# Moving the last pair's first addition, six splits and two copies at the seam of attention and experts

## The chip, the cores and the metric

The kernel runs on one core of a Trainium2 chip. The metric is device microseconds of one execution. The core has TensorE (PE in the rows, PEld for its weight loads), VectorE (DVE), ScalarE (ACT), GpSimd (POOL) and SyncE (SP, which here only issues transfers). Each engine takes its instructions in the order in which they stand, and waits where an operand or a buffer isn't there yet.

## The reference

Attention with bounded scores over 4 batches of 12 heads, then a layer of 8 experts in which each of the 1792 tokens goes to the expert with the largest logit.

```python
# q, k, v: (4, 12, 448, 64); cap = 30
scores = scale * np.matmul(q, k.transpose(0, 1, 3, 2))
scores = cap * np.tanh(scores / cap)
attn = np.exp(scores - max);  attn = attn / (sum(attn) + 1e-09)
out = np.matmul(attn, v)
# x = out, tokens by 768; 8 experts, w1 (768 x 1024), w2 (1024 x 768)
logits = xn @ en.T / tau            # both normalized
expert_idx = np.argmax(logits, axis=1)
probs = softmax(logits);  gate_w = probs[n, expert_idx[n]]
for e in range(E):
    h = np.maximum(x[mask] @ w1[e], 0.0)
    out[mask] = gate_w[mask, None] * (h @ w2[e])
```

## The kernel before

**Attention.** The 48 heads go in 24 pairs, six to a batch. A loop written out by hand runs over pairs `i` (0 to 24) and steps `u` (0 to 3), and what it calls stands in that order on every engine. A step emits the scores of pair `i` for a quarter of the keys (`scores`: PE, then tanh and exp on ACT into `prob`), the product with V of the pair before (`values(i - 1, u)`; at `u == 3` the result is copied out of PSUM as `xt`), pieces of the work that follows a pair (`do_later`), and one piece of `fill`. At `i == 24` there are no scores left, only the values of the last pair, number 23.

**The sums.** The softmax's denominators come from adding up `prob` over the keys' quarters: `add_keys(i)` stands after the four steps of pair `i` and makes `sums` from seven slabs of 448. The first addition (line 792, two slabs to two slabs, 128x896) is on DVE, the rest on POOL; for the last pair one head's rest is on DVE (lines 798, 800), the other's on POOL. `norms` then multiplies `sums` by ones on PE (`d`) and copies the result out as `ds` (line 839); `norms_t` turns it and takes reciprocals; `rows` turns `xt` and scales it into token order (`xsb`, line 866), `router` and `router_t` give the experts' logits (`lp`, `ls`, `lt`, `lgh`).

**The splits.** Experts run in pairs of 16-bit numbers: each 32-bit weight is split in a high part (ACT, line 221) and a low part (DVE, line 222). The first expert is known early, and its 14 pieces of weights (0 to 5 of w1, 6 to 13 of w2), in halves, are the 28 entries of `fill`. A piece comes through a ring of three buffers: after a piece's second half has been split, its buffer is loaded again by SP with the piece three further on (`load_first`, line 694).

**The seam.** After the loop the tokens of the first tile, gathered by POOL (line 198), are turned (`transpose_x`: PE line 212 through `xt`, ACT line 215, DVE line 216; this `xt` is another tile than the pairs'). Then twelve `up` steps follow (line 231, PE: tokens by w1, six steps for each half of the hidden numbers, with `relu` at each half's end), each with one piece of `do_later` and one of `fill`. Then `tile0` makes the down products (line 638, eight groups) with hooks between them: the choice of the expert for the last batch's tokens (`choose`, lines 414 to 422, up to `oh_all`), `count_last` (PE line 443, then the planner's small DVE operations), the gates (lines 427, 428), and `split_until`, which forces what is left of `fill`. After a branch (line 1122) come, on DVE, the order of the experts (`perm` to `pos_e`), the loads of the second expert that hang on it, and the table of all tiles (`bm` line 1216, PE line 1227).

```python
hooks = {2 * DC + f: [lambda n=2 * (5 - f): split_until(n)] for f in range(6)}
hooks[12] += [lambda: choose(last), lambda: all_norms(last)]
hooks[15] += [count_last]
hooks[16] += [lambda: scales_x(last), lambda: gates(last)]
```

Of the kernel before, what the change touches and what calls it, by code (L numbers as in the profile page):

```python
# [30 lines left out]
F32 = mybir.dt.float32  # L31
F32R = mybir.dt.float32r
F16 = mybir.dt.float16
I32 = mybir.dt.int32
AF = mybir.ActivationFunctionType
ALU = mybir.AluOpType
# [3 lines left out]
P = 128  # L40
B, H, S, DH = 4, 12, 448, 64
# [3 lines left out]
E = 8  # L45
# [3 lines left out]
G = 4 * B  # L49
# [31 lines left out]
def attention_moe(ctx: ExitStack, tc: tile.TileContext, q, k, v, cap, emb, tau, w1, w2, qk_pairs, v_pairs, out):  # L81
# [188 lines left out]
    with ExitStack() as actx:  # L270
# [470 lines left out]
        def attention_bounded(apool, ps_s, ps_o):  # L741
# [44 lines left out]
            psum_v = {}  # L786
            sums = {}

            def add_keys(i):
                pt = prob[i]  # L790
                t = apool.tile([P, 2, S], F32, tag="sums", name=f"sums{i}", bufs=3)
                nc.vector.tensor_tensor(t, pt[:, 0:2, :], pt[:, 2:4, :], op=ALU.add)  # L792
                if i < NPAIRS - 1:
                    nc.gpsimd.tensor_tensor(t, t, pt[:, 4:6, :], op=ALU.add)  # L794
                for s in range(2):
                    eng = nc.vector if i == NPAIRS - 1 and s == 0 else nc.gpsimd
                    if i == NPAIRS - 1:
                        eng.tensor_tensor(t[:, s, :], t[:, s, :], pt[:, 4 + s, :], op=ALU.add)
                    sl = slice(s * DH, (s + 1) * DH)
                    eng.tensor_tensor(t[sl, s, :], t[sl, s, :], pt[sl, 6, :], op=ALU.add)  # L800
                sums[i] = t

            def values(i, u):
                vb = loaded[i // 2][1][:, i % 2]
                pt = prob[i]
                if u == 0:
                    psum_v[i] = ps_o.tile([P, 512], F32, tag="v", name=f"v{i}")
                o = psum_v[i]
                if u < 3:
                    for s in range(2):  # L810
                        nc.tensor.matmul(  # L811
                            o[s * DH : (s + 1) * DH, :S],
                            vb[:, u, s * DH : (s + 1) * DH],
                            pt[:, 2 * u + s, :],
                            start=u == 0,
                            stop=False,
                            skip_group_check=True,
                        )
                else:
                    nc.tensor.matmul(  # L820
                        o[:, :S], vb[:, 3, :], pt[:, 6, :], start=False, stop=True, skip_group_check=True
                    )

                if u == 3:
                    x = apool.tile([P, S], F32, tag="xt", name=f"xt{i}", bufs=8)
                    nc.vector.tensor_copy(x, o[:, :S])  # L826
                    xt[i] = x

            xt = {}
# [2 lines left out]
            def norms(i):  # L832

                b, n = i // NP, i % NP
                d = ps_o.tile([P, 512], F32, tag="d", name=f"d{i}")
                for m in range(4):
                    nc.tensor.matmul(d[m * 32 : (m + 1) * 32, :S], ones32, sums[i + m // 2][:, m % 2, :], start=True, stop=True)
                ds = apool.tile([P, S], F32, tag="ds", name=f"ds{i}", bufs=1)
                nc.vector.tensor_copy(ds, d[:, :S])
                return ds  # L840

            def norms_t(i, ds):
# [116 lines left out]
            with tc.manual_schedule():  # L959
                split_qk(0)  # L960
                for i in range(NPAIRS + 1):
                    j = i - 1
                    if i == 0:
                        route.extend(x for f in prepare for x in (f, lambda: None))
                    for u in range(4):
                        if i < NPAIRS:
                            scores(i, u)
                        if (i, u) == (0, 0):
                            split_qk(1)
                        if (i, u) == (0, 1):  # L970
                            warm_up()
                        if u == 2 and 0 < i < NPAIRS - 1:
                            split_qk(i + 1)
                        if j >= 0:
                            values(j, u)
                        if u != 2:
                            do_later()
                        if side:
                            side.pop(0)()
                        if u % 2 == 0 or i >= 3 * NP:  # L980
                            do_route()
                        if u == 1 and len(later) > 2:
                            do_later()
                        if fill and u != 2 and not hold:
                            fill.pop(0)()
                        if hold:
                            hold.pop()
                    if i % 2 == 0 and i // 2 + 2 < NH:
                        load_heads(i // 2 + 2)
                    if i < NPAIRS:  # L990
                        add_keys(i)
                    if j >= 0:
                        after(j)
# [150 lines left out]
    val = work.tile([P, NV, E], F32, tag="val", name="val")  # L1144
    by_pos = work.tile([P, NV, E], F32, tag="by_pos", name="by_pos")
    pos_i = work.tile([1, 2, E], I32, name="pos_i")
    pos_e = work.tile([1, E], I32, name="pos_e")
    perm = work.tile([P, E, E], F32, name="perm")
    table = work.tile([P, NTAB], I32, name="table")
    cp = {}  # L1150
    eid = {}
# [20 lines left out]
    def order():  # L1172
# [4 lines left out]
            place.unsqueeze(1).to_broadcast([P, E, E]),  # L1177
            op=ALU.is_equal,
        )
        which = work.tile([1, E, E], F32, tag="which_e", name="which_e")  # L1180
        nc.vector.tensor_tensor(which, perm[0:1], iota_t[0:1, :E].unsqueeze(1).to_broadcast([1, E, E]), op=ALU.mult)
        with nc.allow_low_precision("numbers of experts, exact"):
            nc.vector.tensor_reduce(pos_e, which, axis=AX.X, op=ALU.add)

    def slots():
        every = work.tile([P, E], F32, tag="every", name="every")
        nc.vector.tensor_tensor(every, done_full, halves, op=ALU.add)
        gn = work.tile([P, E, E], F32, tag="gn", name="gn")
        nc.vector.tensor_tensor(gn, gt, every.unsqueeze(1).to_broadcast([P, E, E]), op=ALU.mult)
        first_t = work.tile([P, E], F32, tag="first_t", name="first_t")  # L1190
        nc.vector.tensor_reduce(first_t, gn, axis=AX.X, op=ALU.add)
        token_rows(last)

        both = work.tile([P, E], F32, tag="both", name="both")
        more = work.tile([P, E], F32, tag="more", name="more")
        nc.vector.scalar_tensor_tensor(out=both, in0=done_full, scalar=-31.0, in1=tails, op0=ALU.add, op1=ALU.mult)
        nc.vector.tensor_tensor(more, first_t, done_full, op=ALU.add)
        nc.vector.tensor_tensor(more, place, more, op=ALU.subtract)
        nc.vector.scalar_tensor_tensor(out=both, in0=both, scalar=32.0, in1=first_t, op0=ALU.mult, op1=ALU.add)
        nc.vector.scalar_tensor_tensor(out=more, in0=more, scalar=float(TAIL0), in1=tails, op0=ALU.add, op1=ALU.mult)  # L1200
        nc.vector.scalar_tensor_tensor(out=both, in0=more, scalar=1024.0, in1=both, op0=ALU.mult, op1=ALU.add)
        at = work.tile([P, G, E], F32, tag="at", name="at")
        nc.vector.tensor_tensor(at, oh_all, both.unsqueeze(1).to_broadcast([P, G, E]), op=ALU.mult)
        slot = work.tile([P, G], F32, tag="slot", name="slot")
        nc.vector.tensor_reduce(slot, at, axis=AX.X, op=ALU.add)
        packed, which, more = [work.tile([P, G], I32, tag=n, name=n) for n in ("packed", "which", "further")]
        nc.vector.tensor_scalar(packed, slot, 31.0 * 32, None, op0=ALU.add)
        nc.vector.tensor_scalar(which, packed, 5, 31, op0=ALU.logical_shift_right, op1=ALU.bitwise_and)
        nc.vector.tensor_scalar(more, packed, 10, None, op0=ALU.logical_shift_right)
# [453 lines left out]
```

## Time and profile before

| | us |
|---|---|
| median of 3 runs (541.33, 545.64, 547.07) | 545.64 |
| the profiled execution | 543.0 |
| its span | 541.3 |
| mean granted clock of TensorE | 0.974 |

Busy shares of the span: PE 88%, DVE 62%, ACT 55%, POOL 44%. Times in the rows count from the span's start; the loop over pairs ends, and the seam begins, some 230 us after it.

### The profile page before, as it was taken

Reading aid. Unit: us, or ns where it says so; the run is one execution under the profiler, and the core shown is the slowest. Engines: PE = TensorE matmul, PEld = TensorE weight load, DVE = VectorE, ACT = ScalarE, POOL = GpSimd, SP = SyncE. Lnnn points to the kernel's source line nnn. Section 1 sums busy time; section 2 is a strip of 40 time slices with the busy share of each in tenths; the row PEclk is TensorE's granted clock in tenths of the full one; section 3 lists DMA queues with packets and bytes.
Section 4 is the critical chain, followed back from the end, with each engine's and each line's share of the span. In section 5 each row is a group of like instructions: output and inputs, shape, how many; then the busy total and the mean of one; then the engine's idle time right before and its main releaser. Section 6 shows DMA issues by size and latency. Waiting matters only on the chain. (4 is left out here: it accounts for less than half of the span.)

```text
span 541.3 us, 11929 instructions
## 1 busy us (share of the span) xinstructions
PE 479.0 (88%) x4597; PEld 311.6 (58%) x4598; DVE 335.4 (62%) x713; ACT 299.7 (55%) x369; POOL 239.2 (44%) x289
## 2 busy tenths in 40 slices
PE   3999998999897988969879699999999999998970
PEld 1444443344433333337658488778887888787760
DVE  4877686968698899587738812591213921396811
ACT  3988788788877987917108301651114811386500
POOL 2567554655553355550125623562333643355321
PEclk9999999999999999979999799999999999999977
DMA  7433219321633540325189911293110952097940
GB/s 224 133 111 114 64 49 312 115 68 45 215 139 130 191 160 0 89 72 178 36 320 401 356 64 59 100 365 115 61 59 32 350 200 72 31 320 256 383 140 11
DMA packets 30514, 83.09 MB, mean 153 GB/s; under 512 B 7277, under 2 KB 7433, under 8 KB 30418
## 3 DMA queue, kind: packets, MB, share of 16 engines
q1 hardware_dynamic: 26354, 67.68, 35.9%
q0 software_dynamic: 2816, 12.61, 6.9%
q10 hardware_dynamic: 1248, 1.64, 0.9%
q8 instruction: 45, 0.74, 0.6%
q14 instruction: 51, 0.42, 0.2%
HBM read 69.51 MB, written 13.00 MB: 152 GB/s over the span
## 5 line engine op out<-in xcount | busy, mean ns | idle before, releaser
L780 ACT ACTIVATE prob<-s,icap 128x896 f32<-128x896 f32 x96 | 86.2, 903 | 25.8 <-PE s L774 18.2
L231 PEld LDWEIGHTS <-h 128*128 128x128 f16 x1056 | 81.5, 100 | 10.3 <-issue 6.6
L794 POOL TENSOR_TENSOR sums<-sums,prob 128x896 f32<-128x896 f32 x23 | 48.3, 2099 | 83.1 <-DVE sums L792 67.5
L784 ACT ACTIVATE prob<-prob,cap_b 128x896 f32<-128x896 f32 (+1 forms) x64 | 81.8, 1277 | 2.1
L231 PE MATMUL h<-xh,h 128*128 128x128 f16 (+1 forms) x480 | 79.6, 220 | 3.1 <-ACT x_tile L669 1.4
L231 PE MATMUL h<-xh,l 128*128 128x128 f16 (+1 forms) x480 | 79.6, 220 | 2.8 <-issue 2.8
L231 PE MATMUL h<-xl,h 128*128 128x128 f16 (+1 forms) x480 | 79.6, 220 | 0.0
L811 PE MATMUL v<-prob,vb 128*64 128x448 f32 x288 | 70.0, 565 | 3.0 <-DVE xt L826 2.9
L800 POOL TENSOR_TENSOR sums<-sums,prob 64x448 f32<-64x448 f32 x47 | 64.3, 1368 | 3.6
L204 POOL TENSOR_TENSOR x_tile<-xg 128x768 f32<-128x768 f32 x16 | 23.5, 1467 | 82.8 <-PE xt L212 72.9
L244 DVE SCALAR_TENSOR_TENSOR hl<-h,hh 128x512 f16<-128x512 f32 (+1 forms) x20 | 13.3, 664 | 65.3 <-ACT hh L243 65.3
L231 PEld LDWEIGHTS <-l 128*128 128x128 f16 x528 | 52.9, 100 | 0.8 <-issue 0.8
L243 ACT ACTIVATE hh<-h 128x512 f16<-128x512 f32 (+1 forms) x20 | 11.5, 574 | 70.1 <-PE h L231 70.1
L215 ACT CAST xh<-xt 128x384 f16<-128x384 f32 x30 | 13.1, 480 | 65.3 <-PE xt L212 57.3
L774 PE MATMUL s<-hi 64*128 64x448 f32 x144 | 34.8, 475 | 15.3 <-DVE hi L756 12.8
L1396 PE MATMUL h<-xh,h 128*128 128x160 f16 x192 | 39.9, 233 | 5.2 <-ACTq L1539 2.6
L638 PEld LDWEIGHTS <-hh 128*128 128x128 f16 (+1 forms) x352 | 32.9, 100 | 19.1 <-issue 0.5
L222 DVE SCALAR_TENSOR_TENSOR l<-w1r,by_pos,h 128x1024 f16<-128x1024 f32 x30 | 37.7, 1307 | 9.5 <-ACT h L221 9.5
L216 DVE TENSOR_TENSOR xl<-xt,xh 128x384 f16<-128x384 f32 x30 | 15.4, 551 | 43.6 <-ACT xh L215 43.5
L774 PEld LDWEIGHTS s<-hi 64*128 64x128 f32 x144 | 14.1, 188 | 47.7 <-ACT prob L780 18.9
L638 PE MATMUL y<-h,hl 128*128 128x384 f16 (+1 forms) x160 | 38.2, 329 | 2.0 <-DVE hl L244 2.0
L1396 PE MATMUL h<-xh,l 128*128 128x160 f16 x192 | 39.9, 233 | 0.0
(315 smaller groups left out, 1135.5 us busy)
## 6 DMA issues: line engine op xcount, KB each, us to landing
w1r<-in_moe_w_dram SPq DMA_DIRECT2D x36, 512.0 KB, 6.1
w2r<-in_moe_w_dram SPq DMA_DIRECT2D x24, 768.0 KB, 8.1
qkb<-in_qk_pairs_dram SPq DMA_DIRECT2D x11, 960.0 KB, 5.7
vb<-in_v_pairs_dram SPq DMA_DIRECT2D x12, 512.0 KB, 6.5
x_dram<-xsb SPq DMA_DIRECT2D x4, 1152.0 KB, 6.7
ring<-in_moe_w_dram SPq DMA_DIRECT2D x6, 512.0 KB, 4.0
ring<-in_moe_w_dram SPq DMA_DIRECT2D x8, 384.0 KB, 3.1
x_dram<-xsb ACTq DMA_DIRECT2D x1, 1152.0 KB
```

Of the source, the lines that this page charges most:

```text
L204: nc.gpsimd.tensor_tensor(x_tile, xg[:, :D], xg[:, SCALE : SCALE + 1].to_broadcast([P, D]), op=ALU.mult)
L216: nc.vector.tensor_tensor(lo, t, hi, op=ALU.subtract)
L222: nc.vector.scalar_tensor_tensor(out=lo, in0=raw, scalar=scale, in1=hi, op0=ALU.mult, op1=ALU.subtract, accum_out=acc)
L231: nc.tensor.matmul(hp[:, f, :W], l[j][:, c], x[:, j, :W], start=j == 0 and f == 0 and n == 0, stop=j == DC - 1 and f == 3 and n == 2, skip ...
L638: nc.tensor.matmul(y, hidden[h][l][:, c, o : o + k], w2p[p % 2][w][f // 2][:, f % 2, m * C : (m + 1) * C], start=f == 0 and n == 0, stop=f ...
L774: nc.tensor.matmul(sp[:, s, :S], l[sl, kc], r[sl, :], start=n == 0, stop=n == 2)
L780: nc.scalar.activation(o, d, AF.Tanh, scale=icap)
L784: nc.scalar.activation(o, o, AF.Exp, scale=cap_b)
L794: nc.gpsimd.tensor_tensor(t, t, pt[:, 4:6, :], op=ALU.add)
L800: eng.tensor_tensor(t[sl, s, :], t[sl, s, :], pt[sl, 6, :], op=ALU.add)
L811: nc.tensor.matmul(o[s * DH : (s + 1) * DH, :S], vb[:, u, s * DH : (s + 1) * DH], pt[:, 2 * u + s, :], start=u == 0, stop=False, skip_grou ...
L1396: nc.tensor.matmul(o, w1p[p % 2][l][j][:, c], x[:, j, :], start=j == 0 and f == fs[0] and m == 0, stop=j == DC - 1 and f == fs[-1] and m == 2,
```

## The change

Four edits. The first addition of pair 23 stands right after its third step of scores, in a function of its own, and no longer after the fourth. Nothing of `fill` is taken at `i == 24`, so three splits are taken later, and at the seam 14 of them are left where it was 11. The copies of pair 23's `xt` and of the last `ds` go from DVE to ScalarE. Some small buffers of the experts' order and table come from the pool `small`, which lasts for the whole program, not from `work`. Lines behind the new function have numbers higher by 4, later by 6.

```diff
--- before.py
+++ after.py
@@ -786,10 +786,15 @@
             psum_v = {}
             sums = {}
 
+            def add_two(i):
+                pt = prob[i]
+                t = sums[i] = apool.tile([P, 2, S], F32, tag="sums", name=f"sums{i}", bufs=3)
+                nc.vector.tensor_tensor(t, pt[:, 0:2, :], pt[:, 2:4, :], op=ALU.add)
+
             def add_keys(i):
-                pt = prob[i]
-                t = apool.tile([P, 2, S], F32, tag="sums", name=f"sums{i}", bufs=3)
-                nc.vector.tensor_tensor(t, pt[:, 0:2, :], pt[:, 2:4, :], op=ALU.add)
+                if i < NPAIRS - 1:
+                    add_two(i)
+                pt, t = prob[i], sums[i]
                 if i < NPAIRS - 1:
                     nc.gpsimd.tensor_tensor(t, t, pt[:, 4:6, :], op=ALU.add)
                 for s in range(2):
@@ -798,7 +803,6 @@
                         eng.tensor_tensor(t[:, s, :], t[:, s, :], pt[:, 4 + s, :], op=ALU.add)
                     sl = slice(s * DH, (s + 1) * DH)
                     eng.tensor_tensor(t[sl, s, :], t[sl, s, :], pt[sl, 6, :], op=ALU.add)
-                sums[i] = t
 
             def values(i, u):
                 vb = loaded[i // 2][1][:, i % 2]
@@ -823,7 +827,7 @@
 
                 if u == 3:
                     x = apool.tile([P, S], F32, tag="xt", name=f"xt{i}", bufs=8)
-                    nc.vector.tensor_copy(x, o[:, :S])
+                    (nc.vector.tensor_copy if i < NPAIRS - 1 else nc.scalar.copy)(x, o[:, :S])
                     xt[i] = x
 
             xt = {}
@@ -836,7 +840,7 @@
                 for m in range(4):
                     nc.tensor.matmul(d[m * 32 : (m + 1) * 32, :S], ones32, sums[i + m // 2][:, m % 2, :], start=True, stop=True)
                 ds = apool.tile([P, S], F32, tag="ds", name=f"ds{i}", bufs=1)
-                nc.vector.tensor_copy(ds, d[:, :S])
+                (nc.vector.tensor_copy if i < NPAIRS - 2 else nc.scalar.copy)(ds, d[:, :S])
                 return ds
 
             def norms_t(i, ds):
@@ -981,10 +985,12 @@
                             do_route()
                         if u == 1 and len(later) > 2:
                             do_later()
-                        if fill and u != 2 and not hold:
+                        if fill and u != 2 and not hold and i < NPAIRS:
                             fill.pop(0)()
                         if hold:
                             hold.pop()
+                        if (i, u) == (NPAIRS - 1, 2):
+                            add_two(i)
                     if i % 2 == 0 and i // 2 + 2 < NH:
                         load_heads(i // 2 + 2)
                     if i < NPAIRS:
@@ -1144,8 +1150,8 @@
     pos_i = work.tile([1, 2, E], I32, name="pos_i")
-    pos_e = work.tile([1, E], I32, name="pos_e")
-    perm = work.tile([P, E, E], F32, name="perm")
+    pos_e = small.tile([1, E], I32, name="pos_e")
+    perm = small.tile([P, E, E], F32, name="perm")
...
-        which = work.tile([1, E, E], F32, tag="which_e", name="which_e")
+        which = small.tile([1, E, E], F32, tag="which_e", name="which_e")
...
-        every = work.tile([P, E], F32, tag="every", name="every")
+        every = small.tile([P, E], F32, tag="every", name="every")
...
-        packed, which, more = [work.tile([P, G], I32, tag=n, name=n) for n in ("packed", "which", "further")]
+        packed, which, more = [small.tile([P, G], I32, tag=n, name=n) for n in ("packed", "which", "further")]
```

On DVE, from the last pair's scores to its additions (`l` is a low part of a split, the numbers are buffers' numbers; ring_178 to ring_180 are the three buffers of the ring), there stands, with - before and + after:

```order
 L222 SCALAR_TENSOR_TENSOR l_154,sums<-ring_178,first_s,h_150 128x384
-L826 COPY xt_2193<-v_2135 128x448
-L897 TENSOR_TENSOR lgh<-lt_2195,inv_2000 128x3x64
-L897 TENSOR_TENSOR lgh<-lt_2195,inv_2000 64x64
+L792 TENSOR_TENSOR sums_2186<-prob_2125 128x896
+L830 COPY xt_2195<-v_2135 128x448
+L901 TENSOR_TENSOR lgh<-lt_2197,inv_2000 128x3x64
+L901 TENSOR_TENSOR lgh<-lt_2197,inv_2000 64x64
 L222 SCALAR_TENSOR_TENSOR l_154,sums<-ring_178,first_s,h_150 128x384
-L792 TENSOR_TENSOR sums_2205<-prob_2125 128x896
-L798 TENSOR_TENSOR sums_2205<-sums_2205,prob_2125 128x448
-L800 TENSOR_TENSOR sums_2205<-sums_2205,prob_2125 64x448
```

The addition of line 792 has moved from behind the second split shown to ahead of the copy of `xt` and of the router's `lgh`; the additions of lines 798 and 800 follow the second split directly (they stand further down, as 803 and 805).

On ACT, at the end of the first expert's splits (`h_153` is the high part of pieces 12 and 13, `hh_211` the second half's relu, `junk` the squares for the tokens' norms, `ex` the exponentials of the gates):

```order
+L221 ACTIVATE h_153<-ring_178,first_s 128x384
+L243 ACTIVATE hh_211<-hp_2251 128x512
+L221 ACTIVATE h_153<-ring_178,first_s 128x384
+L384 ACTIVATE junk_0_2483,den<-xsb 128x768
+L384 ACTIVATE junk_1_2485,den<-xsb 128x768
+L384 ACTIVATE junk_2_2487,den<-xsb 128x768
+L384 ACTIVATE junk_3_2489,den<-xsb 128x768
+L428 ACTIVATE ex<-lg 128x32
 L221 ACTIVATE h_153<-ring_179,first_s 128x384 x2
-L243 ACTIVATE hh_211<-hp_2258 128x512
```

The relu `hh_211` stood behind both halves of pieces 12 and 13 and now stands behind the first half of piece 12; the two halves of piece 13 (ring_179, the unmarked row) stood ahead of the relu, and now stand behind `junk` and `ex`.

## Rows read from the trace of the kernel before

**Rows 1.** Table of stretches: us, busy by PE, PEld, DVE, ACT, POOL, clock, DMA share, GB/s.

```profile
228.00:236.00 8.00, 4.82 (x23) 1.78 (x21) 7.24 (x10) 2.24 (x6) 7.62 (x6) 1.00 0.27 92
236.00:245.00 9.00, 7.58 (x53) 4.51 (x54) 6.25 (x16) 2.34 (x6) 2.21 (x5) 0.62 0.34 89
245.00:252.00 7.00, 7.00 (x117) 6.78 (x115) 5.68 (x21) 4.36 (x9) 0.00 (x0) 1.00 0.57 188
```

**Rows 2.** Timeline of PE, 228 to 246: start, us, [idle before, releaser].

```profile
235.38 0.52 PE L212 MATMUL xt<-ident,x_tile 128*128 128x128 f32 x3 [3.08 <-DVE xsb L866]
236.79 0.72 PE L212 MATMUL xt<-ident,x_tile 128*128 128x128 f32 x3 [0.89 <-DVE xsb L866]
237.44 1.72 PE L837 MATMUL d<-sums,ones 128*32 128x448 f32 x8
...
240.00 0.27 PE L231 MATMUL hp<-xl,h 128*128 128x128 f16 x1 [0.62 <-DVE xl L216]
...
244.45 0.23 PE L231 MATMUL hp<-xh,h 128*128 128x128 f16 x1
...
245.08 0.22 PE L231 MATMUL hp<-xh,l 128*128 128x128 f16 x1
```

**Rows 3.** Timeline of DVE, 222 to 246, same columns.

```profile
224.99 0.62 DVE L222 SCALAR_TENSOR_TENSOR l<-ring,first_s,h 128x384 f16<-128x384 f32 x1 [1.97 <-ACT h L221]
...
226.72 0.62 DVE L826 COPY xt<-v 128x448 f32<-128x448 f32 x1 [1.10 <-PE v L820]
...
228.70 0.99 DVE L222 SCALAR_TENSOR_TENSOR l<-ring,first_s,h 128x384 f16<-128x384 f32 x1 [0.97 <-ACT h L221]
...
229.62 2.01 DVE L792 TENSOR_TENSOR sums<-prob 128x896 f32<-128x896 f32 x1
231.67 1.43 DVE L798 TENSOR_TENSOR sums<-sums,prob 128x448 f32<-128x448 f32 x1
...
234.49 0.74 DVE L866 TENSOR_TENSOR xsb<-xb,inv 128x384 f32<-128x384 f32 x2
```

**Rows 4.** Timeline of POOL, 222 to 240.

```profile
226.06 1.07 POOL L198 DMA_INDIRECT xg<-x_dram,idx_in  x1 [0.28 <-PE s L778]
227.16 2.10 POOL L794 TENSOR_TENSOR sums<-sums,prob 128x896 f32<-128x896 f32 x1
...
234.16 1.39 POOL L800 TENSOR_TENSOR sums<-sums,prob 64x448 f32<-64x448 f32 x1
```

**Rows 5.** Line 792 over the whole trace: ns min/median/max.

```profile
L792 DVE TENSOR_TENSOR sums<-prob x24: 1064/1082/2014, 16.6 to 229.6; 128x896 f32<-128x896 f32 x24
```

**Rows 6.** Timeline of ACT, 222 to 266.

```profile
244.57 0.53 ACT L882 COPY ls<-lp 64x448 f32<-64x448 f32 x1 [5.53 <-PE lp L877]
...
252.19 1.12 ACT L221 ACTIVATE h<-ring,first_s 128x384 f16<-128x384 f32 x2 [0.36 <-DMA ring<-in_moe_w_dram]
...
260.82 0.23 ACT L428 ACTIVATE ex<-lg 128x32 f32<-128x32 f32 x1 [3.30 <-DVE lg L427]
```

**Rows 7.** Line 694, issues of the ring's loads, and their time to landing.

```profile
L694 SPq DMA_DIRECT2D ring<-in_moe_w_dram x8: 332/336/355, 193.2 to 248.3; - x8
...
DMA to landing us min/median/max: 3.1/3.1/3.5
```

**Rows 8.** Timeline of PE, 252 to 276.

```profile
252.54 0.49 PE L638 MATMUL yp<-h,hh 128*128 128x384 f16 x2
...
256.56 0.18 PE L443 MATMUL rp<-oh_all,upper 128*128 128x32 f16 x1 [0.92 <-DVE oh_all L422]
...
272.20 0.56 PE L1227 MATMUL tabp<-bm,a_all 128*128 128x40 f16 x16 [2.81 <-DVE bm L1216]
```

**Rows 9.** Timeline of DVE, 253 to 276.

```profile
254.54 0.85 DVE L414 TENSOR_REDUCE lg<-lgh 128x32 f32<-128x384 f32 x1
...
262.53 0.62 DVE L668 TENSOR_SCALAR x_tile<-yp,gt 128x384 f32<-128x384 f32 x1
```

**Rows 10.** Table of stretches of 3 us around PE's longest wait.

```profile
272.00:275.00 3.00, 1.91 (x40) 1.78 (x40) 2.79 (x14) 0.00 (x0) 1.04 (x2) 1.00 0.81 259
```

More of the change, by code (lines that the diff above doesn't have):

```diff
@@ L1185, in slots @@
     def slots():
-        every = work.tile([P, E], F32, tag="every", name="every")
+        every = small.tile([P, E], F32, tag="every", name="every")
         nc.vector.tensor_tensor(every, done_full, halves, op=ALU.add)
-        gn = work.tile([P, E, E], F32, tag="gn", name="gn")
+        gn = small.tile([P, E, E], F32, tag="gn", name="gn")
         nc.vector.tensor_tensor(gn, gt, every.unsqueeze(1).to_broadcast([P, E, E]), op=ALU.mult)
-        first_t = work.tile([P, E], F32, tag="first_t", name="first_t")
+        first_t = small.tile([P, E], F32, tag="first_t", name="first_t")
         nc.vector.tensor_reduce(first_t, gn, axis=AX.X, op=ALU.add)
         token_rows(last)
-        both = work.tile([P, E], F32, tag="both", name="both")
-        more = work.tile([P, E], F32, tag="more", name="more")
+        both = small.tile([P, E], F32, tag="both", name="both")
+        more = small.tile([P, E], F32, tag="more", name="more")
         nc.vector.scalar_tensor_tensor(out=both, in0=done_full, scalar=-31.0, in1=tails, op0=ALU.add, op1=ALU.mult)
@@ L1201, in slots @@
         nc.vector.scalar_tensor_tensor(out=both, in0=more, scalar=1024.0, in1=both, op0=ALU.mult, op1=ALU.add)
-        at = work.tile([P, G, E], F32, tag="at", name="at")
+        at = small.tile([P, G, E], F32, tag="at", name="at")
         nc.vector.tensor_tensor(at, oh_all, both.unsqueeze(1).to_broadcast([P, G, E]), op=ALU.mult)
-        slot = work.tile([P, G], F32, tag="slot", name="slot")
+        slot = small.tile([P, G], F32, tag="slot", name="slot")
         nc.vector.tensor_reduce(slot, at, axis=AX.X, op=ALU.add)
-        packed, which, more = [work.tile([P, G], I32, tag=n, name=n) for n in ("packed", "which", "further")]
+        packed, which, more = [small.tile([P, G], I32, tag=n, name=n) for n in ("packed", "which", "further")]
         nc.vector.tensor_scalar(packed, slot, 31.0 * 32, None, op0=ALU.add)
```

## The prediction

> **What bounds the kernel now.** I read the table of stretches first. Up to 228 and again from 245 PE is busy nearly all the time; between them lies the seam, where it is not: 4.82 of 8.00 us from 228 to 236 and 7.58 of 9.00 from 236 to 245, these at a mean granted clock of 0.62 [rows 1]. Full speed is 2.4 GHz and the lower level 1.2, so 0.62 over 9 us means some 6.8 us at the lower one (9 x 0.38 / 0.5).
>
> Then PE's timeline says what it waits for. After the last pair's values (ended 232.30) it sits 3.08 us for `xsb` (line 866, DVE), and 0.89 more for the second `xsb`; then the clock is low, and the first `up` step gets its operands at 240.00 [rows 2]. DVE's timeline says why `xsb` is late: from 229.62 to 234.49 DVE adds up pair 23, first the slab addition of line 792 in 2.01 us, then two of 1.43 [rows 3]. So DVE's additions set the start of the seam. POOL's last addition ends at 235.55 (234.16 + 1.39) and is next [rows 4].
>
> The seam's end is set elsewhere. PE starts the down products at 252.54, waits 0.92 for `oh_all` and counts the tokens at 256.56 [rows 8]. Ahead of that stand, back to front, the choice on DVE (from 254.54 [rows 9], so 2.0 us), the relu of the second half, and two splits on ACT that waited for the ring until 252.19 [rows 6]. From the counts all later work follows: DVE's planner, the last down products and their scaling (262.53 [rows 9]), the branch, the table. A step of the seam that gets faster is worth something only as far as the counts and line 668 come earlier.
>
> **The change part by part.**
>
> The first addition. In its new place DVE has 225.62 to 226.72 free (the 1.10 us before the copy of `xt`), and its operands, the first two steps' `prob`, are there. It costs 1.07 at the least, 1.08 in the middle, 2.01 at the most [rows 3, 5]. At 1.07 it ends at 226.7 and costs nothing; at 2.01 it ends at 227.6, and the 0.97 us of idle time before 228.70 take up the rest [rows 3]. What it leaves behind is 2.05 us (229.62 to 231.67): lines 798 and 800 run from 229.62 to 232.4, the first `xsb` is done at 233.3 and PE's turning of tokens begins there, not at 235.38. PE's first wait falls from 3.08 to 1.0 or 1.1. The second `xsb` follows at once, since no split stands between any more: 234.1, not 236.79.
>
> POOL's last addition gets DVE's two-input additions out of its way a bit earlier: it ends between 234.6 (1 us earlier, about half of what DVE gains) and 235.55 as before. I take 234.6, and `d` at 234.7, not at 237.44 [rows 2]. The tokens' low part then needs the cast and the subtraction, with no copy and no split ahead of them on DVE: first `up` step complete at 235.6 where it was 240.00. That is 4.4 us.
>
> The clock. Before, it fell behind the two waits of PE. With one wait of 1.1 us I expect full speed, as in the stretch from 245 to 252 [rows 1]. An `up` step takes 0.67 there (244.45 to 245.08 for its twelve matmuls, and the last one's 0.06) [rows 2]. Twelve are 8.0, and the transposes and the router between them some 2.3 (estimate, at the full clock): 10.3, so they end at 245.9. Before, they went from 240.00 to 252.54, 12.5 us. The down products start 6.6 us earlier.
>
> The splits. Three of them move behind the end of the loop, at 0.56 each on ACT and 0.62 on DVE [rows 3, 6]; both have idle time there (ACT 5.53 in one piece [rows 6]). But the ring's loads hang on them. The buffer of piece 12 is loaded after the second split of piece 9, and that now stands behind the first half's relu and its low part. Six `up` steps (4.0) and what lies between (2.3) end at 241.9; relu, low part and split bring it to 243.8. A load takes 3.1 to 3.5 [rows 7], and the last one took 3.9 (248.3 to 252.19 [rows 6, 7]); with the issue of 0.34, piece 12 is there at 247.4 to 247.7. On ACT the second relu is queued behind its first half (second fence of the change), and behind the relu its low part, the other half's split and the choice: 0.6, 0.6, 0.7, 0.7 and 2.0, with small gaps 4.7 to 4.9. Counts at 252.4, not at 256.56: 4.1 us earlier. So 2.5 of the 6.6 are lost again to the ring. PE has first 3.1 us of down products (252.54 to 255.64 before) and runs dry at 249.0; its wait before the counts grows from 0.92 to 3.4.
>
> The clock again. Behind 3.08 and 0.89 it fell; behind the 2.81 us before the table it did not: the stretch from 272 shows 1.00 [rows 8, 10]. 3.4 is between the two, and nearer to 3.08, so I take that it falls. With the earlier pattern (low from some 1.6 us after the wait, for 6.8 us), 4.3 us of the 5.9 from the counts to line 668 are left when it falls; 3.4 of these take 6.8, and line 668 comes at about 261.6, 0.9 earlier than 262.53.
>
> Piece 13's two splits stand behind `ex` now, some 4.2 us after the counts (260.82 against 256.56 [rows 6, 8]); ACT and DVE finish them 6.1 after the counts, at 258.5. The last of the eight down groups waits for them. With the clock down PE isn't there before, and they cost nothing. With full clock they would set the end: 258.5 and a group of 1.0, line 668 at 259.6, which is 2.9 earlier.
>
> The copies. ScalarE copies as large a tile in 0.53 [rows 6], DVE in 0.62 [rows 3]. The one of `xt` goes on ACT at 232.3, ahead of casts that wait for PE until 233.8; the one of `ds` stands behind the casts, in ACT's idle time. Nothing, at most 0.1 either way.
>
> The pools. No instruction changes. The only wait that does is that of SP's first reading of `pos_e`, now on DVE alone. DVE writes that tile last, so nothing is gained, and nothing lost.
>
> After line 668 everything moves along: DVE's order of experts and `bm` hang on it by the branch, and PE's table on `bm`. Sum: **-0.9 us** on the profiled run of 543.0 (span 541.3), which gives 542.1.
>
> **Rivals.** (1) The clock holds at the counts: -2.9. For it speak the 2.81 us that passed without a fall [rows 8, 10]; against it the fall behind 3.08 and 0.89. (2) The load of piece 12 comes later, and the kernel gets slower. The tokens' write leaves in the same microsecond, and the slowest load shown took 3.9. At 2 us more the counts come only 2.1 earlier, the fall behind them takes its 3.2 (the 4.1 of the forecast less the 0.9 left of it), and the result is +1.1. It decides at 0.9 us beyond 247.7, so from 248.6 on. (3) The seam's start gains nothing, because PE's wait goes on for POOL or DVE, or later waits give it all back: 0. (4) The moved addition gets into POOL's way. In the old place it took 2.01 beside POOL's additions, against 1.08 in the middle [rows 4, 5]; in the new one POOL issues the gather at 226.06 and starts its big addition at 227.16 [rows 4]. If the addition, begun at 225.62, held POOL until 226.7, POOL's chain would be 0.64 later, and `d` with it: 0.6 off the 0.9, so -0.3.
>
> The Trainium skill bears on this ("SBUF — State Buffer", section "Who interferes with whom"): a DVE instruction with two SBUF inputs and a GpSimd instruction that reads SBUF exclude each other, and whichever starts first keeps the shared ports until it ends. By that rule the sum would be rival (4)'s; the doubled duration of line 792 beside POOL agrees with it, and no row shows the addition beside a gather.
>
> **How the numbers follow.** Chances: the forecast 0.50, rival (1) 0.20, rival (2) 0.13, rival (3) 0.12, rival (4) 0.05. A measurement of this kernel can't tell less than about 1% (5.4 us) from no change: its three runs alone lie 5.7 apart. All cases lie within that, so only the spread of the runs can give a difference beyond it: faster 0.09, the same 0.86, slower 0.05. For the time itself: the profiled run less 0.9 is 542.1, the median less 0.9 is 544.7; the mean of the four times known (541.33, 543.0, 545.64, 547.07) is 544.3, less 0.9 is 543.4. I take 543.5. For the range the same mean with -2.9 and +1.1 is 541.4 and 545.4; a median of new runs may lie another 1 or 1.5 off, so 540.4 to 546.8.
>
> **What would show it.** Right: line 792's last instance in about 1.1 us near 226; PE's turning of tokens at 233 to 234 with a wait near 1; clock 1.00 from 236 to 245; the down products at about 246; ACT waiting for the ring until 247.5; the counts near 252.4 after a wait of over 3 us, and a low clock behind it; line 668 near 261.6. Wrong: a clock of 1.00 there and line 668 before 260 (rival 1); the ring until after 248.6 (rival 2); `d` as late as 237 (rival 3); POOL's gather after 226.6 (rival 4). The sum would also be wrong if the order of experts after the branch waited for something else than DVE.

## The result: slower by one per cent, because the last loads of the ring come late

The changed kernel takes 549.36 us (median of 6 runs, 547.23 to 552.24), the kernel before beside it 545.24 (6 runs): a ratio of 1.0101, with a 95% interval of 1.0071 to 1.013. Ratios, here and below, leave out executions more than 1.5 per cent above the fastest of the same kernel and aren't the quotient of the two medians, which can differ from them by up to 0.4 per cent (here it is 1.0076). The forecast was 543.5, range 540.4 to 546.8. It is wrong.

The profiled execution took 547.58, its span is 545.9. Up to the last pair's scores the two traces hold the same instructions but for the moved addition, and yet the changed kernel's is 3.95 us later there: the tanh of pair 23's fourth step starts at 230.79, before at 226.84. Over all traces of this study that point lies between 225.29 and 231.17. So I count from it: "T + 5" is 5 us behind the start of this tanh, whichever trace it is. In the trace before, T is 226.84; there the first turning of tokens stands at T + 8.54, the down products at T + 25.70, the counts at T + 29.72, line 668 at T + 35.69 and the table at T + 45.36.

DVE in the changed kernel's trace, the same stretch and columns as in [rows 3] and [rows 9]:

```profile
229.52 1.08 DVE L792 TENSOR_TENSOR sums<-prob 128x896 f32<-128x896 f32 x1
...
233.19 1.55 DVE L803 TENSOR_TENSOR sums<-sums,prob 128x448 f32<-128x448 f32 x1
234.77 1.44 DVE L805 TENSOR_TENSOR sums<-sums,prob 64x448 f32<-64x448 f32 x1
236.14 1.40 DVE L870 TENSOR_TENSOR xsb<-xb,inv 128x384 f32<-128x384 f32 x4
...
267.25 0.62 DVE L668 TENSOR_SCALAR x_tile<-yp,gt 128x384 f32<-128x384 f32 x1 [0.63 <-PE yp L638]
```

The addition (line 792) takes 1.08 us in its new place, the two others follow the split at once, and `xsb` is done from 236.14 on, T + 5.35 where it was T + 7.65. Line 668 (267.25) is at T + 36.46, 0.8 later than before. PE, to be read against [rows 2] and [rows 8]:

```profile
237.02 1.18 PE L212 MATMUL xt<-ident,x_tile 128*128 128x128 f32 x6 [0.76 <-DVE xsb L870]
238.13 1.27 PE L841 MATMUL d<-sums,ones 128*32 128x448 f32 x8
...
250.25 0.49 PE L638 MATMUL yp<-h,hh 128*128 128x384 f16 x2
...
259.56 0.18 PE L443 MATMUL rp<-oh_all,upper 128*128 128x32 f16 x1 [6.23 <-DVE oh_all L422]
...
259.83 0.80 PE L638 MATMUL yp<-h,hh 128*128 128x384 f16 x2
260.42 0.85 PE L638 MATMUL yp<-l,hh 128*128 128x384 f16 x2
...
276.80 0.56 PE L1233 MATMUL tabp<-bm,a_all 128*128 128x40 f16 x16 [0.30 <-DVE bm L1222]
```

The front did what was forecast. PE waits 0.76 us for the tokens, not 3.08 and 0.89; it turns them at T + 6.23; the down products start at T + 19.46, 6.2 us earlier than before (forecast 6.6). Then it waits 6.23 us for the counts, where it had waited 0.92 and the forecast had 3.4, and the down products behind that take 0.80 to 0.85 us for what took 0.49 at 250.25. Counts at T + 28.77: of the 6.2 us 0.95 are left. At the table (276.80, T + 46.01) the sign has turned. The stretches, to be read against [rows 1]:

```profile
228.00:236.00 8.00, 7.72 (x37) 3.20 (x35) 5.99 (x10) 4.55 (x7) 7.46 (x8) 1.00 0.42 141
236.00:245.00 9.00, 8.09 (x89) 5.50 (x89) 5.63 (x20) 5.09 (x10) 4.33 (x7) 1.00 0.16 46
245.00:252.00 7.00, 7.00 (x104) 6.31 (x102) 5.12 (x18) 3.23 (x6) 0.00 (x0) 1.00 0.76 249
252.00:262.00 10.00, 3.77 (x26) 1.96 (x24) 5.49 (x28) 5.23 (x11) 1.20 (x2) 0.72 0.26 85
```

The clock is 1.00 from 236 to 245, where it was 0.62, and 0.72 from 252 to 262, with PE busy for 3.77 of 10 us. On ACT stands why (the columns of [rows 6]; ACTq is its queue, issuing the tokens' write):

```profile
246.57 0.62 ACTq L407 DMA_DIRECT2D x_dram<-xsb  x1
...
255.20 0.61 ACT L221 ACTIVATE h<-ring,first_s 128x384 f16<-128x384 f32 x1 [5.16 <-DMA ring<-in_moe_w_dram]
255.72 0.58 ACT L243 ACTIVATE hh<-hp 128x512 f16<-128x512 f32 x1
...
263.75 0.23 ACT L428 ACTIVATE ex<-lg 128x32 f32<-128x32 f32 x1 [3.22 <-DVE lg L427]
```

ACT waits 5.16 us for the ring, and the second relu (line 243) stands behind this split. The issues of the ring's last two loads, from SP's timeline, and what line 694 says of that stretch:

```profile
248.32 0.33 SPq L694 DMA_DIRECT2D ring<-in_moe_w_dram  x1
...
249.75 0.33 SPq L694 DMA_DIRECT2D ring<-in_moe_w_dram  x1
...
DMA to landing us min/median/max: 6.4/6.4/6.4
```

They leave at 248.32 and 249.75, behind the tokens' write (1152 KB, 246.57). The 6.4 us are the second one's, piece 13's, the only landing that the view knows in that stretch; the first, piece 12's, ended ACT's wait at 255.20 and so took 6.9. Before, the loads whose landing the view knows, three of the eight, took 3.1 to 3.5 [rows 7], and the last one 3.9 by ACT's wait.

### The profile page after: what moved, and what is told of

Read it like the earlier page. It is cut to its first block, busy times and chain, and to the rows that moved or that the text cites. A ratio compares the mean times of both kernels' runs of the same rounds, so it can differ in the third digit from the quotient of the medians.

```text
span 545.9 us, 11931 instructions
## 1 busy us (share of the span) xinstructions
PE 483.6 (89%) x4597; PEld 313.6 (57%) x4598; DVE 333.5 (61%) x711; ACT 300.9 (55%) x371; POOL 238.7 (44%) x289
## 5 line engine op out<-in xcount | busy, mean ns | idle before, releaser
L815 PE MATMUL v<-prob,vb 128*64 128x448 f32 x288 | 71.6, 576 | 2.5 <-DVE xt L830 2.4
L805 POOL TENSOR_TENSOR sums<-sums,prob 64x448 f32<-64x448 f32 x47 | 62.2, 1324 | 3.6
L1402 PE MATMUL h<-xh,h 128*128 128x160 f16 x192 | 41.1, 237 | 5.2 <-ACTq L1545 2.6
L1402 PE MATMUL h<-xl,h 128*128 128x160 f16 x192 | 41.0, 237 | 0.0
L1402 PE MATMUL h<-xh,l 128*128 128x160 f16 x192 | 41.0, 237 | 0.0
```

Source lines behind the costliest of these rows:

```text
L815: nc.tensor.matmul(o[s * DH : (s + 1) * DH, :S], vb[:, u, s * DH : (s + 1) * DH], pt[:, 2 * u + s, :], start=u == 0, stop=False, skip_grou ...
L1402: nc.tensor.matmul(o, w1p[p % 2][l][j][:, c], x[:, j, :], start=j == 0 and f == fs[0] and m == 0, stop=j == DC - 1 and f == fs[-1] and m == 2,
```

## The experiments

All of them ran with five rounds beside the kernel before; kernels with the same time in the column "before" shared a chip and its runs of the kernel before. Of `e_nofill` the trace of its repeat, `e_nofill2`, is read.

### One part at a time

The four parts alone, each put into the kernel before:

```diff
e_add:   add_two(23) behind the last pair's third step of scores
e_fill:  -  if fill and u != 2 and not hold:
         +  if fill and u != 2 and not hold and i < NPAIRS:
e_copy:  xt23 and ds22 by nc.scalar.copy
e_pool:  pos_e, perm, ... from small
```

> The kernel before with one edit: the first addition of the last pair within its scores. Ring theory (the three postponed splits put the ring's last loads behind the tokens' write, and the counts wait for them): this edit alone is not to blame; the down products start some 4 us earlier, the ring's loads keep their place, the counts come 2 to 4 us earlier and the time falls by 1 to 4 us. Pool theory (the buffers moved to the lasting pool cost the 4 us, from the first pairs on): about the same, -1 to +1 us, or whatever the seam gives. Chance theory (the start lost its 4 us by chance): -1 to +1 us.

> The kernel before with one edit: no splits within the values of the last pair. Ring theory: this is the slow part, +2 to +5 us; a load of the ring takes over 5 us beside the tokens' write, ACT waits for it several us, and PE several us for the counts, with a fall of the clock behind. Pool theory: -1 to +1 us.

> The kernel before with one edit: the copies of the last pair's values and of the last sums on ScalarE. Ring theory: -0.5 to +0.5 us. Pool theory: the same. If it is slower by 2 us or more, both are wrong.

> The kernel before with one edit: the buffers of the experts' order in the lasting pool. Pool theory: +3 to +4 us, already lost before pair 23. Ring theory and chance theory: -0.7 to +0.7 us.

| | median | before | ratio | 95% interval |
|---|---|---|---|---|
| e_add | 542.62 | 543.05 | 0.9995 | 0.9969 to 1.0021 |
| e_fill | 549.57 | 543.05 | 1.0133 | 1.0103 to 1.0163 |
| e_copy | 545.23 | 543.05 | 1.0050 | 1.0024 to 1.0076 |
| e_pool | 542.97 | 543.05 | 1.0006 | 0.9979 to 1.0033 |

The postponed splits alone make the kernel 1.3 per cent slower, more than I had expected of them. The pools do nothing, so the later T of the changed kernel's trace is not theirs. The copies are slower by half a per cent here, 2 us or more, which by what I had written beforehand would speak against both theories (the repeat takes it back); the addition alone is no gain that can be told. The trace of `e_fill` has the pattern of the changed kernel without any of the other parts; PE's counts:

```profile
259.94 0.18 PE L443 MATMUL rp<-oh_all,upper 128*128 128x32 f16 x1 [6.76 <-DVE oh_all L422]
```

and its split on ACT:

```profile
255.59 0.61 ACT L221 ACTIVATE h<-ring,first_s 128x384 f16<-128x384 f32 x1 [5.71 <-DMA ring<-in_moe_w_dram]
```

PE waits 6.76 us, because ACT got the ring's piece 5.71 us late.

### What of the splits it is

```diff
e_nofill: the changed kernel, with
-  if fill and u != 2 and not hold and i < NPAIRS:
+  if fill and u != 2 and not hold:
e_write:  the changed kernel, write_rows(last) not in later, but
+  hooks[15] += [count_last, lambda: write_rows(last, 0, D)]
e_relu:   the changed kernel, in the loop of the up steps
-  if fill:
+  if len(fill) > 4:
e_both:   the edits of e_write and e_relu
```

> The changed kernel with the splits back in the values of the last pair: addition, copies and pools only. Ring theory (the postponed splits are the loss): near the kernel before, -1 to +2 us (the copies alone cost 2, the addition alone nothing). If the addition and the copies together cost 4 us or more, the postponed splits are not the whole cause.

> The changed kernel with the write of the last batch's tokens moved behind the counting, so that the ring's last loads don't run beside its 1152 KB. Contention theory (piece 12's load takes 6.4 instead of 3.1 us because of the write): it lands within 3.1 to 3.5 us, the counts come 3 us earlier, the clock falls less, and the time is 3 to 5 us under that of the changed kernel, about that of the kernel before. Rival (the queue theory: the load is merely issued too late, the write doesn't matter): still over 5 us from issue to landing, time still 4 us over the kernel before.

> The changed kernel with the splits of piece 12 taken behind the second relu and the choice, and only forced by the fifth down group. Order theory (the loss comes from what is queued on ScalarE and VectorE behind the wait for the ring): the load is as slow as in the changed kernel, over 5 us, but PE's wait before the counts falls from 6.2 to at most 2 us, the clock holds there, and the time is 4 to 7 us under that of the changed kernel, at or under the kernel before. Rival (the bytes of the ring are what the end waits for, whatever the order): the wait moves to the seventh down group, and 2 us or less are gained.

> Both edits: the write behind the counting, and piece 12's splits behind the relu and the choice. Both theories: neither the counts nor the seventh down group wait for the ring; 5 to 8 us under the changed kernel, 1 to 3 us under the kernel before. If it is no better than the better of the two, one of the waits was all.

| | median | before | ratio | 95% interval |
|---|---|---|---|---|
| e_nofill | 542.41 | 543.37 | 0.9965 | 0.9936 to 0.9995 |
| e_write | 545.03 | 543.37 | 1.0034 | 1.0002 to 1.0066 |
| e_relu | 541.55 | 543.37 | 0.9926 | 0.9897 to 0.9954 |
| e_both | 543.21 | 543.37 | 0.9986 | 0.9960 to 1.0012 |

Without the postponed splits the rest of the change is no loss. In `e_write` the last two loads still take 4.8 to 4.9 us, though the write is gone from there and nothing but loads of the ring is under way; issued 1.1 us apart, the two are in each other's way (2.0 us apart, in `e_pool` and `e_nofill2`, they took 2.8 to 3.2). The write is therefore a part, 2.0 of the 3.8 us by which piece 12's load exceeds the usual 3.1, and with it gone the counts come at T + 26.80 after a wait of 4.25, and the time is 0.3 per cent over the kernel before and no longer 1.0 or more. Neither theory was quite right: contention, but with each other too. Line 694 in that stretch of `e_write`:

```profile
L694 SPq DMA_DIRECT2D ring<-in_moe_w_dram x2: 332/332/333, 246.6 to 247.7; - x2
...
DMA to landing us min/median/max: 4.8/4.8/4.9
```

In `e_relu` the loads are as slow as ever (7.1 and 6.6), but only the last down groups wait for them. The counts come at T + 24.15, after 0.37 us, on PE:

```profile
250.93 0.18 PE L443 MATMUL rp<-oh_all,upper 128*128 128x32 f16 x1 [0.37 <-DVE oh_all L422]
```

and the split on ACT:

```profile
252.64 1.12 ACT L221 ACTIVATE h<-ring,first_s 128x384 f16<-128x384 f32 x2 [0.65 <-DMA ring<-in_moe_w_dram]
```

So the slow loads alone cost little; the loss comes from what was queued behind them, the relu, the choice and the counts. How far `e_relu` lies under the kernel before is less sure than its ratio: the two medians give 0.9966. Both edits together gave no more than one of them, and can't be told from the kernel before; I had expected 1 to 3 us under it.

### The clock, the copies, and the changed kernel again

```diff
e_same:   the changed kernel
e_warm:   the changed kernel, on PE ahead of the counts
+  for _ in range(24):
+      nc.tensor.matmul(d, ones16, a_all[:, 0:4, :], start=True, stop=True)
e_nocopy: the changed kernel, both copies by nc.vector.tensor_copy
e_best:   e_relu, both copies by nc.vector.tensor_copy
```

> The changed kernel once more, as a standard on this chip: +4 to +6 us over the kernel before; in its trace the ring's last two loads take over 6 us and PE waits over 5 us for the counts. If the time is within 2 us of the kernel before, the first comparison was chance.

> The changed kernel with 24 matmuls of no use (128x512, some 5 us) on PE ahead of the counts, in the wait for them. Clock theory (of the loss, 2 us or more are the lower clock that follows that wait): the clock stays at 1.00 through the down products, last down product to counts back from 7.2 to about 5.5 us, time 1.5 to 3 us under that of the changed kernel. Rival (only the wait itself counts): no change, -0.5 to +0.5 us.

> The changed kernel with the two copies back on VectorE. If the cost of the copies alone (+2.2 us, measured on the kernel before) adds to that of the splits: 2 to 3 us under the changed kernel. If it came from splits queued behind the waiting copies on ScalarE, which the changed kernel no longer has there: within 1 us of the changed kernel.

> The changed kernel with piece 12's splits behind the second relu and the choice, and the copies on VectorE. It was 4 us under the kernel before with the copies on ScalarE. If the copies cost by themselves, 5 to 7 us under the kernel before; if not, 3 to 5.

| | median | before | ratio | 95% interval |
|---|---|---|---|---|
| e_same | 547.99 | 541.26 | 1.0120 | 1.0087 to 1.0153 |
| e_warm | 548.24 | 541.26 | 1.0126 | 1.0085 to 1.0168 |
| e_nocopy | 546.56 | 541.26 | 1.0081 | 1.0053 to 1.0110 |
| e_best | 542.52 | 541.26 | 1.0021 | 0.9998 to 1.0045 |

The loss repeats. `e_warm` is the answer on the clock at the counts, which I had in the forecast with over 3 us. PE's timeline of it:

```profile
253.06 5.34 PE L1019 MATMUL keep<-a_all,ones 128*128 128x512 f16 x24
259.47 0.18 PE L443 MATMUL rp<-oh_all,upper 128*128 128x32 f16 x1 [1.07 <-DVE oh_all L422]
...
259.72 0.48 PE L638 MATMUL yp<-h,hh 128*128 128x384 f16 x2
...
264.88 0.32 PE L638 MATMUL yp<-h,hh 128*128 128x384 f16 x1 [0.18 <-ACT h L221]
...
265.57 0.32 PE L638 MATMUL yp<-l,hh 128*128 128x384 f16 x1 [0.21 <-DVE l L222]
265.74 0.48 PE L638 MATMUL yp<-h,hl 128*128 128x384 f16 x2
```

The useless matmuls fill the wait (24 in 5.34 us), and the down products behind it take 0.49 from the first on: the clock held. From the counts to the last down product 6.27 us pass, where `e_same` has 7.28 and the changed kernel 7.17. And yet the time is no better. The last down group waits for the splits of piece 13 (0.18 and 0.21 us), PE starts the next tile behind the branch, and the table follows DVE: from the counts to the table 16.7 us in `e_warm`, 17.2 and 17.3 in the two others. By the traces some 0.6 us of the loss are the clock behind this wait, and the times show no gain (1.0126 against 1.0120, each known to some 2 us): the 2 us or more of the clock theory aren't there. In `e_nocopy` the loads take 7.3 and 6.8 us, PE waits 6.63 for the counts, and most of the loss stays; it isn't the copies. `e_best` was to be 3 to 5 us under the kernel before and isn't under it at all (see the repeats).

### The bytes earlier: a fourth buffer, and repeats

```diff
e_ring4:  the changed kernel
-  ring_w = [... for i in range(3)]
+  ring_w = [... for i in range(4)]
-  load_first(e, i + 3)
+  load_first(e, i + 4)
   ... (`piece` and the first loads with 4 in place of 3)
e_relu2, e_best2, e_nofill2, e_copy2, e_add2: the kernels without the 2, again
```

> The changed kernel with four buffers in the ring instead of three, so that the load of piece 12 hangs on piece 8's split and not on piece 9's. Ring theory (the loss is that this load is issued behind the tokens' write, and all that is queued behind it): it is issued some 3.5 us earlier, ahead of the write, and takes 3.1 to 3.5 us; PE's wait for the counts falls from 6.3 to at most 1.5 us; the time is 4 to 8 us under that of the changed kernel, at or under the kernel before. Rival (the loss is in the three splits themselves, that have to be done later, wherever the bytes are): at most 2 us are gained.

> The changed kernel with piece 12's splits behind the relu and the choice, once more, beside its twin with the copies on VectorE. If the 4 us under the kernel before were real: 2 to 5 us under it again. If chance: within 1 us of it.

> The same with the copies on VectorE, on the same chip as its twin. If ScalarE is the better place for the copies in this order: 3 to 5 us over the twin, as the first two measurements on different chips had it. If the place of the copies doesn't matter: within 1.5 us of the twin.

> The changed kernel with the splits back in the last pair's values, once more: its first profile was disturbed. 1 to 3 us under the kernel before if the addition gives what the profile shows (PE's wait for the tokens 1.5 to 2 us shorter); within 1 us if that is taken up by the counts.

> The copies alone, once more. If ScalarE's waiting copies really cost: +1.5 to +3 us again. If the first +2.2 was the spread between measurements, of the size that the twins showed: -1 to +1 us.

> The addition alone, once more, on the same chip. With the splits in the values, addition, copies and pools together gave -2 and -3 us. If the addition is the gain in that: -1 to -4 us; if not, -1 to +1 us, as the first time.

| | median | before | ratio | 95% interval |
|---|---|---|---|---|
| e_ring4 | 541.47 | 543.90 | 0.9959 | 0.9928 to 0.9989 |
| e_relu2 | 543.71 | 543.90 | 0.9980 | 0.9949 to 1.0012 |
| e_best2 | 539.29 | 543.90 | 0.9897 | 0.9853 to 0.9942 |
| e_nofill2 | 540.53 | 543.90 | 0.9925 | 0.9892 to 0.9958 |
| e_copy2 | 543.41 | 542.90 | 1.0010 | 0.9988 to 1.0031 |
| e_add2 | 542.50 | 542.90 | 0.9981 | 0.9951 to 1.0010 |

With a fourth buffer, and the three splits as late as in the changed kernel, the loss is gone. Piece 12's load now leaves at 244.01, ahead of the write (245.78). The view below knows the landing of none but the load at 241.1. The trace's own record of landings (each load raises a semaphore in sixteen parts) has piece 12's last part at 247.09, 3.1 us after its issue. Piece 13's load leaves at 247.54, behind the write, and its last part lands at 254.13: 6.6 us, as slow as in the changed kernel, and nothing waits for it. ACT doesn't wait for the ring at all, and PE waits 1.10 for the counts. PE of `e_ring4`:

```profile
253.65 0.18 PE L443 MATMUL rp<-oh_all,upper 128*128 128x32 f16 x1 [1.10 <-DVE oh_all L422]
```

Line 694 in the stretch of its last loads, and half a microsecond of the table of stretches (columns of [rows 1]) in which 387 GB/s are still under way, after 250.6, when a load of 3.1 us would have been there:

```profile
L694 SPq DMA_DIRECT2D ring<-in_moe_w_dram x3: 333/333/333, 241.1 to 247.5; - x3
...
DMA to landing us min/median/max: 3.1/3.1/3.1
...
251.50:252.00 0.50, 0.50 (x5) 0.30 (x4) 0.50 (x3) 0.47 (x2) 0.00 (x0) 1.00 0.95 387
```

This settles the cause: not the splits, but the late load of piece 12 and the queue behind it. The expected 4 to 8 us under the changed kernel are met (0.9959 against 1.0101 and 1.0120, some 8 us). All kernels with the postponed splits fall in line by ACT's wait for piece 12: 5.2 to 5.7 us in the changed kernel, `e_same`, `e_warm`, `e_nocopy` and `e_fill`, which are 0.8 to 1.3 per cent over the kernel before; 3.7 us in `e_write`, 0.3 per cent over it; at most 0.65 us in `e_relu`, `e_best`, `e_both`, `e_ring4` and the repeats, from 1.0 per cent under it to 0.2 over.

The repeats are a lesson about size. `e_relu` and `e_best` differ only in the place of two copies; by the ratios the first was 0.95 per cent better when each was beside its own standard, and 0.83 per cent worse when both were on one chip. The copies alone were +0.5 and then +0.1 per cent, the addition alone -0.05 and -0.2. `e_best` alone came out 1.2 per cent apart (1.0021 and 0.9897). So effects of under half a per cent or so, 3 us, and now and then of more, aren't told apart here by one measurement, though each had an interval of some 0.3 to either side. What stands on two measurements of one sign: the changed kernel (+1.0 and +1.2 per cent), and the change without the postponed splits (`e_nofill`, -0.35 and -0.75, both intervals under 1). That is the best candidate for a version that beats both kernels.

## Why the prediction was wrong

**What bounds the kernel, and the front.** Right: DVE's additions did set the start of the seam. Line 792 took 1.08 (forecast 1.07), PE's wait 0.76 (1.0 to 1.1), the clock held, the down products began 6.2 us earlier (6.6). In other executions the front gave less: the turning of tokens begins at T + 6.23 in the changed kernel, `e_add` and `e_add2`, but at T + 8.06 to 9.11 in `e_nofill2`, `e_ring4` and `e_same`; what decides it stands at rival (4).

**The failed step** is the price of the load: "A load takes 3.1 to 3.5, and the last one took 3.9; with the issue of 0.34, piece 12 is there at 247.4 to 247.7." It was issued at T + 17.53 (forecast 243.8, T + 16.96), took 6.9, and ACT had it at T + 24.41 (forecast T + 20.9 at the latest). I took the duration from loads that had left ahead of the write, 2 us or more apart (and the 3.1 to 3.5 from the three of eight whose landing the view knew), and put it on one that left behind the write with another 1.4 us after it. The write was named only in rival (2), which got 0.13. Everything else at the counts follows: a wait of 6.23 and not 3.4, counts 0.95 earlier and not 4.1. Rival (2) was the right mechanism.

**Its size.** Rival (2) gave +1.1, with 2 us more for the load; it was some 3.5 more. Behind the counts the forecast was too dear instead: 3.2 us more up to line 668, by the lower clock, with everything after it moving along. The table comes 17.2 to 17.3 us behind the counts in the changed kernel, 15.5 to 15.8 in the traces without postponed splits (`e_add`, `e_copy`, `e_pool`, `e_nofill2`, the kernel before): 1.6 us. Of these some 0.6 are the clock; where it holds, in `e_warm` and `e_ring4`, 16.7 and 16.8 remain, with piece 13's splits behind `ex`, which I had let cost nothing while the clock is down. And the trace of before was no typical standard: `e_pool`, whose instructions stand in the same order, has its counts at T + 26.43, 3.3 us earlier than the kernel before, with a shorter fall of the clock in the seam. So the front had less to win than one profile showed.

**The sum of the runs.** Counts: T + 28.77, 31.23 and 29.26 in the changed kernel, `e_same` and `e_nocopy`, mean 29.75; T + 29.72, 26.43, 27.62 and 29.12 in the kernel before, `e_pool`, `e_copy` and `e_copy2`, mean 28.2. That is 1.5, with the 1.6 behind the counts some 3.1 us. Measured were 1.0 and 1.2 per cent, 5.5 and 6.5 us. What is missing, 2 to 3 us, isn't settled by one profile for each kernel; on the average T itself lies 1.5 us later in the five traces with the slow seam (the three named, `e_fill` and `e_warm`: 229.2) than in seven without postponed splits (227.7), though up to there the order differs in the moved addition at most. The seven other traces with the postponed splits, whose order up to T is the changed kernel's, have 227.9, so the order isn't the cause; it may be chance in so few traces, and stays open.

**The clock at the counts** did fall, as forecast, and cost some 0.6 us where I had 3.2. The ground for the forecast was weak: 3.4 us isn't "between the two" waits named, 2.81 and 3.08, but beyond both. **The last splits** behind `ex` did hold the last down group when the clock held, as forecast (0.18 and 0.21 us in `e_warm`). **The copies** cost nothing that two measurements agree on (the 0.53 us taken for ScalarE are of a tile half as large; the moved copy of 128x448 took 0.53 too), **the pools** nothing.

**Rival (4)**: in the changed kernel's trace the gather wasn't delayed; it took 1.08 us beside the addition. In six of the other traces with the moved addition (`e_best`, `e_both`, `e_relu`, `e_relu2`, `e_nofill2`, `e_ring4`) it was. There POOL comes to the copy of the gather's indices only when the addition has just begun, and the copy lasts 1.06 us and not 0.17, as here in `e_ring4`:

```profile
227.46 1.08 DVE L792 TENSOR_TENSOR sums<-prob 128x896 f32<-128x896 f32 x1
...
227.53 1.06 POOL L197 COPY idx_in<-idx 128x1 int32<-128x1 int32 x1
...
228.86 1.07 POOL L198 DMA_INDIRECT xg<-x_dram,idx_in  x1 [0.28 <-ACT prob L780]
```

The gather leaves at T + 0.1 to 0.9, in the changed kernel's trace at T - 1.34; DVE's next addition (line 803) waits for POOL's behind the gather, and the tokens are turned at T + 7.5 to 8.3 and not at 6.2. Some 0.9 us of that are the copy's, more than the 0.6 of rival (4), which got 0.05. In two further traces the addition itself was held, as told below.

## What to carry to other kernels

When a piece of work is postponed, follow what it gives free: here three splits of half a microsecond each held a buffer, the buffer's load slipped behind a large write, and the load's duration more than doubled. Take a transfer's duration from transfers with the same neighbours, not from the median. And look at what stands in the queue behind an instruction that may wait for memory: moving piece 12's two splits behind the relu and the choice, or giving the ring one more buffer, took the loss away with the loads as they were or with the splits as they were.

## What the runs showed of the hardware

An addition of two SBUF tiles on VectorE can be held far beyond the doubling that the kernel before showed. In `e_same`, the changed kernel's second trace, POOL's gather came 0.6 us earlier against T. The moved addition there, on DVE:

```profile
228.60 3.50 DVE L792 TENSOR_TENSOR sums<-prob 128x896 f32<-128x896 f32 x1
```

and POOL beside it:

```profile
227.96 1.07 POOL L198 DMA_INDIRECT xg<-x_dram,idx_in  x1 [0.28 <-POOL idx_in L197]
229.06 2.09 POOL L799 TENSOR_TENSOR sums<-sums,prob 128x896 f32<-128x896 f32 x1
```

It lasted 3.50 us, against 1.08 in the changed kernel's first trace, and ended 0.95 us after POOL's addition of 2.09 (229.06 to 231.15). The copy of `xt` stood behind it, and PE waited 2.50 us for that in the values of the last pair; the gain of the front was lost in that execution (tokens at T + 9.11). In `e_warm` it lasted 3.56 us, in the same place beside POOL's. So the moved addition was free in most traces and cost over 2 us in these two, by which engine came first.

The old place shows the same end. Before, an addition of POOL's (line 800) ran from 229.34 to 230.68, and DVE's of 2.01 us (229.62) ended at 231.63 [rows 3]. In all seven traces in which the last addition was held (the kernel before, `e_copy`, `e_copy2`, `e_fill`, `e_pool`, `e_same`, `e_warm`) it ended 0.95 to 0.96 us after POOL's, nearly its whole usual 1.08, whether it began behind POOL's (by 0.27 to 0.47 us) or ahead of it (by 0.46 and 0.52). So the start that the profile gives need not be the moment at which the addition gets its operands; that is a reading of the rows, and no run tests it.

"SBUF — State Buffer" of the Trainium skill, section "Who interferes with whom", says that of two such instructions the one that starts first keeps the shared ports until it ends. That one is held by the other for so long agrees with it; that it is the addition, which begins 0.46 us ahead of POOL's by the rows, doesn't.
